# Two hand-outs counted one row group sooner, and raw weights in pieces, in a fused attention and top-1 mixture kernel

## The chip, the core and the metric

The kernel runs on one core of one Trainium2 chip. TensorE multiplies, VectorE (DVE), ScalarE (ACT) and GpSimd (POOL) do the elementwise work, SyncE (SP) and GpSimd issue the transfers between HBM and the core's memory. Each engine and each issuing queue works its own list in order; a row that waits holds everything behind it on that engine. The metric is device time in microseconds (us), the median of several runs; lower is better.

## The reference

Two stages, one behind the other. First an attention over the columns of q, k and v (4 batches of 5056 x 256, the columns of q and k normalised over the 5056 rows), then a mixture of 8 experts over the resulting 20224 tokens, each token going to the one expert with the largest logit.

```
qn = q / (norm(q, axis=1) + 1e-06);  kn = k / (norm(k, axis=1) + 1e-06)
s = kn.T @ qn / tau;  a = softmax(s, -1);  x = v @ a          # per batch, s is 256 x 256
e_idx = argmax(x @ w_gate, axis=1)
gate_w = softmax(x @ w_gate)[e_idx];  eom = sigmoid(x @ w_output_gate)
for e in range(8):
    mask = e_idx == e
    h = relu(x[mask] @ w1[e])                                  # 256 -> 1024
    out[mask] = gate_w[mask] * eom[mask, e] * (h @ w2[e])      # 1024 -> 256
```

## The kernel before

**Stages.** For each of the four batches b, `gram(b)` builds k'q in 20 steps: a step loads two 256 KB pieces into one buffer (tag "qk", six buffers), TensorE multiplies them (s_ps), ACT squares them and DVE adds the squares up; its tail normalises and does the softmax. `mix(b)` then multiplies v with the result, in five row groups (NG = 5) of four steps: v comes in 512 KB pieces (tag "v", four buffers), TensorE transposes it (vt_ps), ACT and DVE split it into a high and a low part (vh, vl), three matmuls give x_ps, and ACT copies that into st (tag "st", four buffers, one per group). `route` decides each token's expert (r_oh and the counts r_ps) and scatters the rows of st from GpSimd into xs_d in HBM, region by expert, eight scatters a group. The mixing of one batch runs beside the gram of the next.

**Units.** Tokens of one expert are worked off in units of 256 (`blocks`): `fetch_x` reads the rows of a unit into xg (which takes a buffer of tag "qk"), `prepare` copies the token numbers (b_id), scales, splits into two f16 parts (xr) and transposes by DMA (xt); then come the matmuls of h_ps with the relu's hb, and those of y_ps, and GpSimd scatters the result to the output. hb shares the tag "raw" with raw weights of the first two ranks. There are 14 early units (FEW = 4 and 10), the others are made when all tokens are counted.

**Hand-outs.** `checkpoint(0)` after the second mixing and `checkpoint(1)` after the third hand out units of the tokens so far; `checkpoint(2)` hands out the rest. The first part of each ranks the experts by their counts (`rank_experts`, the row numbers ri) and issues a *mark*: a small read of xs_d from GpSimd that waits for the scatters before it, and for which every x fetch of these units waits (`open_marks`). The second part makes the tables of units.

**Weights.** `prep(first, end)` works through the ranks: `gather` asks SyncE for the 1 MB of raw weights of one half (w1 or w2) of the rank's expert, and `split` squares it on ACT for a scale (L297), splits it into two f16 parts (L310 on ACT, L311 on DVE) and stores both parts in HBM (wsc, L316). Rank 0 stays in wbuf as well; units from FIRST[1] = 4 on fetch the weights of their rank into wbuf from GpSimd (L825). Raw weights of ranks 0 and 1 have buffers of their own ("raw"), ranks 2 to 7 use those of st. FIRST[r] is the first unit that can have rank r, worked out from the tokens that are sure to be counted.

**Order.** The program is written as generators that the driver at the end steps beside each other: a mixing step, then so many steps of gram (GRATE), of weights (PRATE, MRATE, WRATE) and of units (BRATE). From that the scheduler sets each engine's list. In the third mixing units start at its step OPEN = 10, when the tables were finished at step LATE = 5.

Of the kernel before, what the change touches and what calls it, by code (L numbers as in the profile page):

```python
# [20 lines left out]
P = 128  # L21
# [23 lines left out]
def tile_colnorm_attention_then_top1_moe(  # L45
# [42 lines left out]
    assert 0 < EARLY and LATER >= NHALF  # L88


    sure = [-(-(n * N - E * (BLK - 1)) // BLK) for n in (SOON, B - 1)]
    FIRST = [-(-r * sure[0] // E) for r in range(AHEAD + 1)]
    FIRST += [
        FIRST[AHEAD] - (FIRST[AHEAD] - sure[1]) * (r - AHEAD) // (E - AHEAD) for r in range(AHEAD + 1, E)
# [36 lines left out]
    RLATE = 2  # L131
    GRATE = 1.3
    PRATE = 1.2
    DEEP, LAG, REST = 2, 3, 2
    LATE, OPEN, MARKED = 5, 10, 3
    FAR, NEAR = 5, 1
    BRATE = 0.7
    DRY = 4
    MRATE = 1.2
    WRATE = 0.8  # L140
    units = []
    after = mybir.DependencyInfo(mybir.DependencyClass.Sync, mybir.DependencyReason.DATA)
    xs_d = dr.tile([NSLOT + P, CW], I32, name="xs_d")
# [113 lines left out]
    def prep(first, end):  # L257
        jobs = [(r, half) for r in range(first, end) for half in range(2)]
        raws = []

        def gather():
            r, half = jobs[len(raws)]
            if r > AHEAD:
                raw = wk.tile([P, R, CW], F32, tag="st", name=f"raw{r}_{half}", bufs=STB)
                raw = raw.rearrange("p r w -> p (r w)")[:, :HW1]
            else:
                raw = big.tile([P, HW1], F32, tag="raw", name=f"raw{r}_{half}", bufs=3)
            row = nc.values_load(
                ri[0:1, r : r + 1], engines=[mybir.EngineType.SP], min_val=0, max_val=(E - 1) * P,
                skip_runtime_bounds_check_because="rows of the weights of an expert",  # L270
            )
            if half == 0:
                nc.sync.dma_start(raw, wraw[0][bass.ds(row, P), :])
            else:
                rows = wraw[1][bass.ds(row, P), :].rearrange("(f a) (b d) -> (a b) f d", f=FC, d=C)
                nc.sync.dma_start(raw.rearrange("p (f d) -> p f d", f=FC), rows)
            raws.append(raw)

        for n, (r, half) in enumerate(jobs):
            while len(raws) < min(n + DEEP, len(jobs)):  # L280
                gather()
                yield
            yield from pause(LAG if n == 0 else REST)
            yield from split(raws[n], half, r)

    def split(raw, half, r):

        rows = slice(r * P, (r + 1) * P)
        if r == 0:
            hi, lo = (wbuf[half][:, 0, n * HW1 : (n + 1) * HW1] for n in range(2))  # L290
        else:
            hi = big.tile([P, HW1], F16, tag="sp", name=f"whi{r}_{half}", bufs=1)
            lo = big.tile([P, HW1], F16, tag="sl", name=f"wlo{r}_{half}", bufs=1)
        ss = sm.tile([P, 2], F32, tag="wss", name="wss")
        for i in range(2):
            a = slice(i * HW1 // 2, (i + 1) * HW1 // 2)
            nc.scalar.activation(hi[:, a], raw[:, a], AF.Square, accum_out=ss[:, i : i + 1])  # L297
# [9 lines left out]
        src, dh, dl = raw, hi, lo  # L307
        cuts = [(slice(None), slice(i * HW1 // 2, (i + 1) * HW1 // 2)) for i in range(2)]
        for i, a in enumerate(cuts):
            nc.scalar.activation(dh[a], src[a], AF.Copy, scale=sw)  # L310
            nc.vector.scalar_tensor_tensor(  # L311
                out=dl[a], in0=src[a], scalar=sw, in1=dh[a], op0=ALU.mult, op1=ALU.subtract
            )
            yield
        for n, part in enumerate((hi, lo)):
            nc.sync.dma_start(wsc[half][rows, n * HW1 : (n + 1) * HW1], part)  # L316
# [135 lines left out]
    sowing = []  # L452
    left = [None]

    def mix(b):
        later = None
        turned = []
        sts = {}
# [36 lines left out]
        for j in range(total):  # L495
            g, i = divmod(j, R // 2)
            if j + AHD < total:
                turn(j + AHD)
            if i == 0:
                st = wk.tile([P, R, CW], F32, tag="st", name=f"st{b}_{g}", bufs=STB)  # L500
            vh, vl = turned.pop(0)
            for t in range(2):
                x_ps = ps_x.tile([P, 512], F32, tag="x", name="x_ps")
                for c in range(CC):
                    tsl = slice(t * P, (t + 1) * P)
                    nc.tensor.matmul(x_ps[:, :CW], vh[:, c, tsl], ah[:, c, :], start=c == 0, stop=False)  # L506
                    nc.tensor.matmul(x_ps[:, :CW], vh[:, c, tsl], al[:, c, :], start=False, stop=False)  # L507
                    nc.tensor.matmul(x_ps[:, :CW], vl[:, c, tsl], ah[:, c, :], start=False, stop=c == CC - 1)  # L508
                left[0] = nc.scalar.copy(st[:, 2 * i + t, :], x_ps[:, :CW])  # L509
            sow(1)  # L510
            if i == RLATE and later:
                next(later)
                sowing.append(later)
                sow(1)
            yield
            if i == R // 2 - 1:
                later = route(b, g, st)
                next(later)
        yield
        yield  # L520
        sow(R)
        finish(later)
        yield

# [248 lines left out]
    def checkpoint(ck):  # L773
        last = ck == len(FEW)
        if last:
            close_regions()
        else:
            rank_experts(ck > 0)
        of_rank(rcr, rc)
        open_marks(ck)  # L780
        yield
        if not last:
            a = len(units)
            z = a + FEW[ck]
            table(BLK, FEW[ck], lambda row: [(row[:, a:z], lambda r: r)])
            weights(a, z)
            new = [2] * FEW[ck]
        else:

            few = NHALF - TAIL  # L790
            lead = LATER - few
            mid, end = EARLY + lead, NUNIT - TAIL

            def pairs(a):
                return a[:, mid:end].rearrange("p (h s) -> p h s", s=2)

            def fulls(a):
                return [(a[:, EARLY:mid], lambda r: r[:, :lead]), (pairs(a)[:, :, 0], lambda r: r[:, lead:])]

            def halves(a):  # L800
                return [(pairs(a)[:, :, 1], lambda r: r[:, :few]), (a[:, end:], lambda r: r[:, few:])]

            table(BLK, LATER, fulls)
            table(BLK // 2, NHALF, halves)
            weights(EARLY, NUNIT)
            nc.vector.tensor_copy(more_i, used[0:1, end : end + 1])
            new = [2] * lead + [2, 1] * few + [1] * TAIL
        for nt in new:
            u = len(units)
            units.append(dict(nt=nt, ck=ck, gi=gi[:, u : u + 1], wi=wi[:, u : u + 1], top=max(r for r in range(E) if FIRST[r] <= u)))  # L810
# [153 lines left out]
    def blocks(a, z):  # L964
# [11 lines left out]
        while g <= z:  # L976
# [18 lines left out]
            for fp, steps in enumerate(ORDER):  # L995
# [6 lines left out]
                        y_part(g - 1, part)  # L1002
                if fp == 1:
                    adv("prep", prepare, g + 1 + XP)
                if fp == 0 and a == 0 and g == z - DRY:
                    tc.keep_in_program_order(nc.gpsimd.drain())
                yield
# [14 lines left out]
    for _ in grams[0]:  # L1022
        for _ in range(PER_STAGE):
            next(ahead)
    run = blocks(0, NUNIT - TAIL)
    for b in range(SOON):
        _beside(mix(b) if b else first, (ahead, GRATE))
        while b + 1 not in a_of:
            next(ahead)
    some = checkpoint(0)  # L1030
    next(some)
    preps = prep(0, AHEAD)
    for b in range(SOON, B - 1):
        for i, _ in enumerate(_steps(mix(b), (ahead, GRATE), (preps, PRATE))):
            if i == LATE:
                finish(some)
                opened[0] += 1
            if i >= OPEN:
                next(run)
        while b + 1 not in a_of:  # L1040
            next(ahead)
            next(run)
    finish(preps)
    some = checkpoint(1)
    next(some)
    preps = prep(AHEAD, E)
    for i, _ in enumerate(_steps(mix(B - 1), (run, BRATE), (preps, MRATE))):
        if i == LATE:
            finish(some)
        if i == LATE + MARKED:  # L1050
            opened[0] += 1
    finish(checkpoint(2))
    for i, _ in enumerate(_steps(run, (preps, WRATE))):
        if i == MARKED:
            opened[0] += 1

    more = nc.values_load(
# [34 lines left out]
```

## Time and profile before

| what | us |
|---|---|
| median of three runs | 1208.28 (1202.16 to 1210.1) |
| the profiled execution | 1209.88 |
| its span | 1208.1 |
| mean granted clock of TensorE in it | 0.990 |
| TensorE busy | 1174.4 |
| last matmul of the mixing (L506) starts; units alone behind it | 387.3 |

The span is what the trace covers. Busy time of TensorE takes in matmuls at a lower granted clock, so a stretch can be busy and still lose time. How the span looks in 40 slices (tenths of busy time; the clock in tenths; DMA the busy share of the transfer engines):

```
PE   8999999997997999999999999999999999999997
DVE  7787768788685966566666654555554555555531
ACT  6576656576574555555556443333333444344432
POOL 0003756536565753333444433344444444444433
PEclk9999999999998998999999999999999999999999
DMA  9976888877767898657554436643325534336533
```

A slice is 30 us. The stages of attention fill the first thirteen, the units, from 296 us on, the others beside and behind them.

### The profile page before, as it was taken

The page shows a single profiled execution, that of the slowest core. Times are in us where ns is not written, and L with a number is a line of the kernel's source. Part 1 is how long each engine was busy: PE and PEld are TensorE (multiplying, and loading weights), DVE is VectorE, ACT ScalarE, POOL GpSimd, SP SyncE. Part 2 cuts the span into 40 slices and gives each one's busy share as a digit, 9 for nine tenths or more (in the row PEclk, how much of TensorE's full clock was granted, in tenths as well). Part 3 has the DMA queues.
Part 4 walks back from the last instruction along what each step waited for, and adds up shares of the span by engine and source line. Part 5 has one row for each costly group of instructions (what it writes and reads, how often), then busy time and mean ns, then how long its engine had stood idle before and what let it go on. Part 6 is the DMA issues. An engine that isn't in the chain of part 4 may idle for free.

```text
span 1208.1 us, 28097 instructions
## 1 busy us (share of the span) xinstructions
PE 1174.4 (97%) x10412; PEld 1066.4 (88%) x10412; DVE 748.5 (62%) x2300; ACT 602.3 (50%) x1193; POOL 517.9 (43%) x518
## 2 busy tenths in 40 slices
PE   8999999997997999999999999999999999999997
PEld 7899999887996888888888888888889999999997
DVE  7787768788685966566666654555554555555531
ACT  6576656576574555555556443333333444344432
POOL 0003756536565753333444433344444444444433
PEclk9999999998998999999999999999999999999999
DMA  9976888877767898657554436643325534336533
GB/s 319 330 246 207 301 277 259 295 242 215 212 242 236 223 264 178 150 147 174 148 137 126 112 80 113 182 76 77 72 63 176 112 73 82 79 81 197 168 104 130
DMA packets 186307, 208.56 MB, mean 173 GB/s; under 512 B 121832, under 2 KB 134510, under 8 KB 182200
## 3 DMA queue, kind: packets, MB, share of 16 engines
q1 hardware_dynamic: 145368, 139.41, 42.0%
q0 software_dynamic: 40512, 67.05, 18.9%
q8 instruction: 84, 1.38, 0.5%
q14 instruction: 55, 0.45, 0.1%
q10 hardware_dynamic: 288, 0.26, 0.1%
HBM read 281.84 MB, written 61.41 MB: 284 GB/s over the span
## 4 chain that ended last, share of the span: by engine, by line
PE 87%; DMA 6%; DVE 2%; issue 2%; ACT 1%; SPq 1%; POOL 0%; POOLq 0%; DVEq 0%; ACTq 0%
PE h_ps L919 11%; PE h_ps L921 11%; PE h_ps L920 11%; PE y_ps L942 11%; PE y_ps L943 11%; PE y_ps L944 11%; PE s_ps L366 10%; PE x_ps L506 3%; PE x_ps L508 2%; PE x_ps L507 2%; PE vt_ps L477 2%; DMA wbuf<-wsc,wi 1%; DMA qk<-in_k_dram 1%; DMA raw<-in_moe_w_dram 1%; DMA qk<-in_q_dram 1%
## 5 line engine op out<-in xcount | busy, mean ns | idle before, releaser
L924 DVE SCALAR_TENSOR_TENSOR hb<-h_ps,hb 128x512 f16<-128x512 f32 (+1 forms) x360 | 228.5, 636 | 276.0 <-ACT hb L923 275.1
L923 ACT ACTIVATE hb<-h_ps 128x512 f16<-128x512 f32 (+1 forms) x360 | 197.9, 552 | 364.1 <-PE h_ps L921 362.5
L919 PE MATMUL h_ps<-xt,wbuf 128*128 128x256 f16 (+1 forms) x1440 | 366.5, 262 | 3.0 <-ACT st L509 3.0
L921 PE MATMUL h_ps<-xt,wbuf 128*128 128x256 f16 (+1 forms) x1440 | 366.6, 262 | 0.0
L920 PE MATMUL h_ps<-xt,wbuf 128*128 128x256 f16 (+1 forms) x1440 | 366.5, 262 | 0.0
L942 PE MATMUL y_ps<-wbuf,hb 128*128 128x256 f16 x1296 | 353.3, 273 | 5.0 <-ACT yo L948 2.4
L944 PE MATMUL y_ps<-wbuf,hb 128*128 128x256 f16 x1296 | 353.3, 273 | 0.0
L943 PE MATMUL y_ps<-wbuf,hb 128*128 128x256 f16 x1296 | 353.3, 273 | 0.0
L825 POOL DMA_INDIRECT wbuf<-wsc,wi x172 | 177.8, 1034 | 404.5 <-PE h_ps L921 365.2
L598 POOL DMA_INDIRECT xs_d<-st,r_si x160 | 168.1, 1051 | 199.2 <-DVE r_d L550 101.9
L954 POOL DMA_INDIRECT out_dram<-yo,b_id x162 | 165.4, 1021 | 69.2 <-issue 42.3
L366 PE MATMUL s_ps<-qk 128*128 128x256 f32 x640 | 152.4, 390 | 5.8 <-DMA qk<-in_q_dram 3.9
L920 PEld LDWEIGHTS <-wbuf 128*128 128x128 f16 x1440 | 141.0, 98 | 16.9 <-issue 3.2
L919 PEld LDWEIGHTS <-wbuf 128*128 128x128 f16 x1440 | 142.1, 99 | 14.1
L921 PEld LDWEIGHTS <-wbuf 128*128 128x128 f16 x1440 | 141.1, 98 | 13.3
L943 PEld LDWEIGHTS <-hb 128*128 128x128 f16 x1296 | 126.8, 98 | 19.3 <-issue 5.6
L366 PEld LDWEIGHTS s_ps<-qk 128*128 128x128 f32 x640 | 121.4, 196 | 21.2 <-DMA qk<-in_k_dram 3.9
L944 PEld LDWEIGHTS <-hb 128*128 128x128 f16 x1296 | 126.8, 98 | 14.9
L942 PEld LDWEIGHTS <-hb 128*128 128x128 f16 x1296 | 126.8, 98 | 14.3
L354 DVE TENSOR_TENSOR acc<-acc,sq 128x1024 f32<-128x1024 f32 x76 | 92.9, 1223 | 46.8 <-ACT sq L353 45.4
L880 ACT ACTIVATE xr<-xg,b_sx 128x256 f16<-128x256 f32 x162 | 74.6, 502 | 66.8 <-DVE b_sx L233 46.4
L353 ACT ACTIVATE sq<-qk 128x1024 f32<-128x1024 f32 x76 | 80.3, 1060 | 53.0 <-DMA qk<-in_k_dram 44.8
(191 smaller groups left out, 1448.8 us busy)
## 6 DMA issues: line engine op xcount, KB each, us to landing
xg<-xs_d SPq DMA_DIRECT2D x72, 272.0 KB
qk<-in_q_dram SPq DMA_DIRECT2D x75, 256.0 KB
qk<-in_k_dram SPq DMA_DIRECT2D x75, 256.0 KB
v<-in_v_dram SPq DMA_DIRECT2D x32, 512.0 KB
raw<-in_moe_w_dram SPq DMA_DIRECT2D x16, 1024.0 KB
wsc<-whi SPq DMA_DIRECT2D x14, 512.0 KB
wsc<-wlo SPq DMA_DIRECT2D x14, 512.0 KB
v<-in_v_dram SPq DMA_DIRECT2D x8, 480.0 KB
```

The source lines that it names most:

```text
L366: nc.tensor.matmul(s_ps[:, c, :], kt[:, 1, t, c * P : (c + 1) * P], qt[:, 0, t, :], start=st == 0 and t0 == 0 and t == 0 and c == 0 and n ...
L598: ins = nc.gpsimd.indirect_dma_start(out=xs_d[:, :], out_offset=bass.IndirectOffsetOnAxis(ap=si[:np_, t : t + 1], axis=0), in_=st[:np_, t, ...
L825: nc.gpsimd.indirect_dma_start(out=wbuf[half][:, at_of(u), :], out_offset=None, in_=wsc[half][:end, :], in_offset=bass.IndirectOffsetOnAxi ...
L919: nc.tensor.matmul(hp, w1s[:, 0, c, fs], xh, start=fi == 0 and c == 0, stop=False, **KWM)
L920: nc.tensor.matmul(hp, w1s[:, 0, c, fs], xl, start=False, stop=False, **KWM)
L921: nc.tensor.matmul(hp, w1s[:, 1, c, fs], xh, start=False, stop=fin, **KWM)
L923: nc.scalar.activation(hh, h_ps[:, :, :w], AF.Relu)
L924: nc.vector.scalar_tensor_tensor(out=hb[:, 1, 2 * fp : 2 * fp + 2, :w], in0=h_ps[:, :, :w], scalar=0.0, in1=hh, op0=ALU.max, op1=ALU.subtract,
L942: nc.tensor.matmul(y_ps[:, t, :], hb[:, 0, f, tsl], w2s[:, 0, f, :], start=st, stop=False, **KWM)
L943: nc.tensor.matmul(y_ps[:, t, :], hb[:, 0, f, tsl], w2s[:, 1, f, :], start=False, stop=False, **KWM)
L944: nc.tensor.matmul(y_ps[:, t, :], hb[:, 1, f, tsl], w2s[:, 0, f, :], start=False, stop=fin, **KWM)
L954: ins = nc.gpsimd.indirect_dma_start(out=out[:, :], out_offset=bass.IndirectOffsetOnAxis(ap=un["id"][:, t : t + 1], axis=0), in_=un["yo"][ ...
```

## The change

- `sure` (from which FIRST follows) takes off one batch's last row group, 960 tokens. FIRST goes from 0, 4, 11, 18, 25, 32, 39, 46 to 0, 4, 11, 17, 23, 30, 36, 42.
- `mix` takes a hook. In the second and third mixing it ranks the experts when the last row group's third step runs, and issues the mark at the end of the mixing, ahead of the last group's scatters. The hand-outs so count four of the five groups of their last batch.
- The tables are finished at step 1 of the next mixing (LATE) and units start at step 3 (OPEN). Weights of rank 0 start in the second mixing at step 18 (HOOKED), those of rank 1 in the third one at step 18; rank 2 and later wait 22 steps more (REST_AT), and pause four steps a half (SLOW).
- Raw weights come in two transfers a half, the f16 parts go out in two stores each, with steps of other work between. Ranks 2 to 7 use buffers of tag "v" in place of "st".
- `blocks` calls `fetch_x` at every step.

```diff
-    sure = [-(-(n * N - E * (BLK - 1)) // BLK) for n in (SOON, B - 1)]
+    sure = [-(-(n * N - (N - (NG - 1) * GROUP) - E * (BLK - 1)) // BLK) for n in (SOON, B - 1)]
...
-    DEEP, LAG, REST = 2, 3, 2
-    LATE, OPEN, MARKED = 5, 10, 3
+    DEEP, LAG, REST, SLOW = 2, 4, 1, 4
+    LATE, OPEN, MARKED, HOOKED = 1, 3, 3, 18
...
-    BRATE = 0.7
+    REST_AT = 22
+    BRATE = 0.72
...
-    MRATE = 1.2
-    WRATE = 0.8
+    MRATE = 1.8
+    WRATE = 1.0
...
             if r > AHEAD:
-                raw = wk.tile([P, R, CW], F32, tag="st", name=f"raw{r}_{half}", bufs=STB)
-                raw = raw.rearrange("p r w -> p (r w)")[:, :HW1]
+                parts = [
+                    ld.tile([P, 4, C], F32, tag="v", name=f"raw{r}_{half}_{i}", bufs=VB).rearrange("p t c -> p (t c)")
+                    for i in range(2)
+                ]
             else:
                 raw = big.tile([P, HW1], F32, tag="raw", name=f"raw{r}_{half}", bufs=3)
+                parts = [raw[:, i * HW1 // 2 : (i + 1) * HW1 // 2] for i in range(2)]
...
+            for i, part in enumerate(parts):
+                if half == 0:
+                    nc.sync.dma_start(part, rows[:, i * HW1 // 2 : (i + 1) * HW1 // 2])
...
+                yield
...
-            yield from pause(LAG if n == 0 else REST)
+            yield from pause(LAG if n == 0 else SLOW if r > AHEAD + 1 else REST)
...
-        for n, part in enumerate((hi, lo)):
-            nc.sync.dma_start(wsc[half][rows, n * HW1 : (n + 1) * HW1], part)
+            for n, part in enumerate((hi, lo)):
+                nc.sync.dma_start(wsc[half][rows, n * HW1 + a.start : n * HW1 + a.stop], part[:, a])
+            yield
...
+                if g == NG - 1 and hook:
+                    next(hook)
...
         sow(R)
+        if hook:
+            next(hook)
         finish(later)
...
         of_rank(rcr, rc)
+        if not last:
+            yield
         open_marks(ck)
...
+                adv("x", fetch_x, got["prep"] + QKB)
...
     for b in range(SOON, B - 1):
-        for i, _ in enumerate(_steps(mix(b), (ahead, GRATE), (preps, PRATE))):
+        for i, _ in enumerate(_steps(mix(b, hand[1]), (ahead, GRATE))):
+            if i < HOOKED:
+                due += PRATE
+                while due >= 1.0:
+                    due -= 1.0
+                    next(preps, None)
+            else:
+                if i == HOOKED:
+                    finish(preps)
+                    preps = chain(prep(AHEAD, AHEAD + 1), pause(REST_AT), prep(AHEAD + 1, E))
+                next(preps)
             if i == LATE:
-                finish(some)
+                finish(hand[0])
                 opened[0] += 1
             if i >= OPEN:
-                next(run)
+                some += 1.0 if i < OPEN + FAR + XP + 1 + NEAR else BRATE
```

The matmuls stay the same, in number and shape; the lists of the engines change order. Three places show it.

The first is GpSimd's queue at the end of the second mixing; st_4 is its last row group, the st_0 behind it the first of the third mixing. Before:

```order
L598 DMA xs_d<-st_3_2251,r_si 163968x272 x8
L598 DMA xs_d<-st_4_2439,r_si 163968x272 x8
L615 DMA mark<-xs_d 128x1
L598 DMA xs_d<-st_0_2766,r_si 163968x272 x8
L598 DMA xs_d<-st_1_2954,r_si 163968x272 x8
```

After:

```order
L608 DMA xs_d<-st_3_2251,r_si 163968x272 x8
L625 DMA mark<-xs_d 128x1
L608 DMA xs_d<-st_4_2439,r_si 163968x272 x8
L608 DMA xs_d<-st_0_2778,r_si 163968x272 x8
L608 DMA xs_d<-st_1_3020,r_si 163968x272 x8
```

The mark has moved ahead of eight scatters. In SyncE's queue in the same place, raw_0 and raw_1 are the two halves of rank 0's raw weights, qk_15 the loads of gram step 15 of the last batch. Before:

```order
L342 DMA qk_15_3165<-in_q_dram 128x512
L342 DMA qk_15_3165<-in_k_dram 128x512
L268 TENSOR_LOAD ri
L273 ISA
L273 DMA raw_0_2793<-in_moe_w_dram 128x2048
L268 TENSOR_LOAD ri
L276 ISA
L276 DMA raw_1_2833<-in_moe_w_dram 128x8x256
L342 DMA qk_16_3243<-in_q_dram 128x512
L342 DMA qk_16_3243<-in_k_dram 128x512
```

After (the last of four fetches of token rows, and what follows it; the four pieces of raw weights stand a little ahead, behind qk_10):

```order
L851 TENSOR_LOAD gi
L855 ISA
L855 DMA xg<-xs_d 128x544
L348 DMA qk_11_3037<-in_q_dram 128x512
L348 DMA qk_11_3037<-in_k_dram 128x512
L348 DMA qk_12_3073<-in_q_dram 128x512
L348 DMA qk_12_3073<-in_k_dram 128x512
L471 DMA v_3_2_3537<-in_v_dram 128x1024
L471 DMA v_4_0_3641<-in_v_dram 120x1024
L321 DMA wsc_85<-wbuf_155 128x1024 x2
L348 DMA qk_13_3149<-in_q_dram 128x512
L348 DMA qk_13_3149<-in_k_dram 128x512
```

Rank 0's raw weights have gone from behind step 15 to behind step 10; the fetches of token rows, which came behind step 19, come ahead of step 11, and rank 0's stores (wsc) between the later steps, two of them ahead of 13, two ahead of 14, one ahead of 16 and three ahead of 17.

The second place is DVE in the first row group of the third mixing, around r_oh, on which r_ps waits. Before (the tb_ rows and elist make the table of units):

```order
L552 SCALAR_TENSOR_TENSOR r_val<-r_d,c_113 128x64
L571 CAST st_0_2766<-ids 128x8
L701 TENSOR_REDUCE tb_res<-tb_pr 128x4 x2
L554 TENSOR_REDUCE r_mv<-r_val 128x8
L714 SCALAR_TENSOR_TENSOR tb_ex<-tb_res,tb_g_3035 128x4
L704 SCALAR_TENSOR_TENSOR tb_sl<-jf,tb_res 128x4
L556 TENSOR_TENSOR r_oh<-r_val,r_mv 128x64
```

After:

```order
L581 CAST st_0_2778<-ids 128x8
L489 TENSOR_TENSOR vl<-vt_ps,vh 128x512
L564 TENSOR_REDUCE r_mv<-r_val 128x8
L871 COPY b_id<-xg 128x2
L875 TENSOR_REDUCE b_mx<-xg 128x2
L571 TENSOR_REDUCE r_se<-r_d 128x8
L566 TENSOR_TENSOR r_oh<-r_val,r_mv 128x64
L871 COPY b_id<-xg 128x2
L875 TENSOR_REDUCE b_mx<-xg 128x2
L232 TENSOR_SCALAR b_mx<-b_mx 128x2
L489 TENSOR_TENSOR vl<-vt_ps,vh 128x512
```

The first rows of unit 0 (b_id, which reads a fetched xg) now stand ahead of r_oh, and unit 1's ahead of the next vl; units 2 and 3 follow within ten rows. In the last mixing, four b_id stand ahead of the first vl in the same way.

The third place is SyncE in the last mixing, at the raw weights of rank 2. Before:

```order
L268 TENSOR_LOAD ri
L276 ISA
L276 DMA raw_1_5208<-in_moe_w_dram 128x8x256
L839 TENSOR_LOAD gi
L843 ISA
L843 DMA xg<-xs_d 128x544
L839 TENSOR_LOAD gi
L843 ISA
L843 DMA xg<-xs_d 128x544
L885 DMA_TRANSPOSE xt<-xr_3657 128x4x128 x4
L316 DMA wsc_86<-whi_1_4850 128x2048
L316 DMA wsc_86<-wlo_1_4851 128x2048
```

After:

```order
L855 DMA xg<-xs_d 128x544
L321 DMA wsc_85<-whi_0_4392 128x1024 x2
L471 DMA v_3_2_5076<-in_v_dram 128x1024
L321 DMA wsc_85<-wlo_0_4393 128x1024 x2
L471 DMA v_4_0_5218<-in_v_dram 120x1024
L471 DMA v_4_2_5377<-in_v_dram 120x1024
L321 DMA wsc_86<-whi_1_4599 128x1024 x2
L321 DMA wsc_86<-wlo_1_4600 128x1024 x2
L897 DMA_TRANSPOSE xt<-xr_3296 128x4x128 x2
L273 TENSOR_LOAD ri
L280 ISA
L280 DMA raw_0_0_5686<-in_moe_w_dram 128x1024
```

The raw weights of rank 2 (raw_1_5208 is the second half of them, raw_0_0_5686 the first piece of their first half) have gone behind the stores of rank 1 (wsc) and behind the last loads of v.

More of the change, by code (lines that the diff above doesn't have):

```diff
@@ L263, in gather @@
             if r > AHEAD:
-                raw = wk.tile([P, R, CW], F32, tag="st", name=f"raw{r}_{half}", bufs=STB)
-                raw = raw.rearrange("p r w -> p (r w)")[:, :HW1]
+                parts = [
+                    ld.tile([P, 4, C], F32, tag="v", name=f"raw{r}_{half}_{i}", bufs=VB).rearrange("p t c -> p (t c)")
+                    for i in range(2)
+                ]
             else:
                 raw = big.tile([P, HW1], F32, tag="raw", name=f"raw{r}_{half}", bufs=3)
+                parts = [raw[:, i * HW1 // 2 : (i + 1) * HW1 // 2] for i in range(2)]
+            raws.append(parts)
             row = nc.values_load(
@@ L271, in gather @@
             )
[L272 to L277, printed above, removed]
+            rows = wraw[half][bass.ds(row, P), :]
+            for i, part in enumerate(parts):
+                if half == 0:
+                    nc.sync.dma_start(part, rows[:, i * HW1 // 2 : (i + 1) * HW1 // 2])
+                else:
+                    nf = FC // 2
+                    of = rows.rearrange("(f a) (b d) -> (a b) f d", f=FC, d=C)[:, i * nf : (i + 1) * nf, :]
+                    nc.sync.dma_start(part.rearrange("p (f d) -> p f d", f=nf), of)
+                yield
         for n, (r, half) in enumerate(jobs):
             while len(raws) < min(n + DEEP, len(jobs)):
-                gather()
-                yield
-            yield from pause(LAG if n == 0 else REST)
+                yield from gather()
+            yield from pause(LAG if n == 0 else SLOW if r > AHEAD + 1 else REST)
             yield from split(raws[n], half, r)
@@ L296, in split @@
             a = slice(i * HW1 // 2, (i + 1) * HW1 // 2)
-            nc.scalar.activation(hi[:, a], raw[:, a], AF.Square, accum_out=ss[:, i : i + 1])
+            nc.scalar.activation(hi[:, a], raw[i], AF.Square, accum_out=ss[:, i : i + 1])
             yield
@@ L305, in split @@
         root2(tot, KW, sw, invw[:, half, r : r + 1])
[L307 to L310, printed above, removed]
+        for i in range(2):
+            a = slice(i * HW1 // 2, (i + 1) * HW1 // 2)
+            nc.scalar.activation(hi[:, a], raw[i], AF.Copy, scale=sw)
             nc.vector.scalar_tensor_tensor(
-                out=dl[a], in0=src[a], scalar=sw, in1=dh[a], op0=ALU.mult, op1=ALU.subtract
+                out=lo[:, a], in0=raw[i], scalar=sw, in1=hi[:, a], op0=ALU.mult, op1=ALU.subtract
             )
+            for n, part in enumerate((hi, lo)):
+                nc.sync.dma_start(wsc[half][rows, n * HW1 + a.start : n * HW1 + a.stop], part[:, a])
             yield
-        for n, part in enumerate((hi, lo)):
-            nc.sync.dma_start(wsc[half][rows, n * HW1 : (n + 1) * HW1], part)
         if half == 1:
@@ L453, in tile_colnorm_attention_then_top1_moe, with mix @@
     left = [None]
-    def mix(b):
+    def mix(b, hook=None):
         later = None
@@ L1025, in tile_colnorm_attention_then_top1_moe @@
     run = blocks(0, NUNIT - TAIL)
+    hand = [checkpoint(n) for n in range(len(FEW))]
+    preps = prep(0, AHEAD)
     for b in range(SOON):
-        _beside(mix(b) if b else first, (ahead, GRATE))
+        hook = hand[0] if b == SOON - 1 else None
+        for i, _ in enumerate(_steps(mix(b, hook) if b else first, (ahead, GRATE))):
+            if hook and i >= HOOKED:
+                next(preps)
         while b + 1 not in a_of:
             next(ahead)
-    some = checkpoint(0)
-    next(some)
-    preps = prep(0, AHEAD)
+    due = some = 0.0
     for b in range(SOON, B - 1):
-        for i, _ in enumerate(_steps(mix(b), (ahead, GRATE), (preps, PRATE))):
+        for i, _ in enumerate(_steps(mix(b, hand[1]), (ahead, GRATE))):
[4 more added lines that the diff above has]
+                    next(preps, None)
+            else:
+                if i == HOOKED:
+                    finish(preps)
+                    preps = chain(prep(AHEAD, AHEAD + 1), pause(REST_AT), prep(AHEAD + 1, E))
+                next(preps)
             if i == LATE:
-                finish(some)
+                finish(hand[0])
                 opened[0] += 1
             if i >= OPEN:
-                next(run)
+                some += 1.0 if i < OPEN + FAR + XP + 1 + NEAR else BRATE
+                while some >= 1.0:
+                    some -= 1.0
+                    next(run)
         while b + 1 not in a_of:
@@ L1042, in tile_colnorm_attention_then_top1_moe @@
             next(run)
[L1043 to L1046, printed above, removed]
     for i, _ in enumerate(_steps(mix(B - 1), (run, BRATE), (preps, MRATE))):
         if i == LATE:
-            finish(some)
+            finish(hand[1])
         if i == LATE + MARKED:
@@ L1053, in tile_colnorm_attention_then_top1_moe @@
     for i, _ in enumerate(_steps(run, (preps, WRATE))):
-        if i == MARKED:
+        if i == 3:
             opened[0] += 1
```

## The prediction, made before the changed kernel ran

> **What bounds the kernel now.** I read the page first: busy shares and the chain that ended last.
>
> ```profile
> PE 1174.4 (97%) x10412; PEld 1066.4 (88%) x10412; DVE 748.5 (62%) x2300; ACT 602.3 (50%) x1193; POOL 517.9 (43%) x518
> ...
> PE 87%; DMA 6%; DVE 2%; issue 2%; ACT 1%; SPq 1%; POOL 0%; POOLq 0%; DVEq 0%; ACTq 0%
> ```
>
> TensorE is the bound almost everywhere. The change removes no matmul, so it can only move the places where TensorE stands. Those I found with a table by stretches (PE busy, count, granted clock, DMA share, GB/s):
>
> ```profile
> 238.00:250.00 12.00, 7.91 (x46) 0.86 0.80 291
> 250.00:274.00 24.00, 24.00 (x176) 1.00 0.78 247
> 274.00:296.00 22.00, 14.84 (x112) 0.84 0.82 211
> 366.00:384.00 18.00, 10.44 (x64) 0.81 0.85 259
> 420.00:430.00 10.00, 8.36 (x77) 1.00 0.99 227
> ...
> 430.00:1184.00 754.00, 753.75 (x7311) 1.00 0.51 126
> ```
>
> Behind 430 us nothing is to be won: 753.75 of 754 us are busy. Four stretches ahead of it lose time. I count idle time plus busy time times the missing share of the clock: 4.1 + 1.1 = 5.2 us at 238, 7.2 + 2.4 = 9.5 at 274, 7.6 + 2.0 = 9.5 at 366 and 1.6 at 420. That is 25.8 us, the whole stake. The waits of TensorE in these stretches name the releasers:
>
> ```profile
> PE r_ps L576 <- DVE r_oh L556: 5.3, 1, 5.3
> PE r_ps L576 <- ACT st L509: 4.1, 1, 4.1
> ...
> PE h_ps L919 <- ACT st L509: 3.0, 1, 3.0
> PE y_ps L942 <- ACT yo L948: 2.4, 1, 2.4
> PE vt_ps L477 <- DVE vl L483: 2.1, 1, 2.1
> PE y_ps L942 <- DMA wbuf<-wsc,wi: 1.6, 1, 1.6
> ```
>
> The names on ACT and DVE are not the causes. The chain of waits shows what each had been standing behind. At 238 us:
>
> ```profile
> 229.36 0.60 DVE vl L483
> 231.09 8.47 DMA raw<-in_moe_w_dram
> 239.59 2.19 ACT wbuf L297 x4
> ...
> 242.50 0.28 ACT st L509
> ```
>
> Rank 0's raw weights are asked for at 231.09 and land at 239.56; the squares of L297 stand on ACT ahead of the copy into st, so ACT, and then TensorE, wait for the weights. At 366 us it is SyncE's queue (its rows in order of time), held first by the longest of its waits at L276:
>
> ```profile
> SPq L276 <- DMA xs_d<-st,r_si: 18.5, 2, 9.4
> ...
> 358.11 0.39 SPq L276 DMA_DIRECT2D raw<-in_moe_w_dram  x1
> 359.05 1.23 SPq L843 DMA_DIRECT2D xg<-xs_d  x2
> 360.39 9.85 SPq L885 DMA_TRANSPOSE xt<-xr  x4
> 370.34 0.53 SPq L316 DMA_DIRECT2D wsc<-whi  x1
> ...
> 370.34 6.91 DMA wsc<-whi
> 377.33 0.13 ACT whi L297
> ```
>
> The raw weights of rank 2 go into an st buffer whose scatters have not landed. SyncE stands 9.4 us; the rows of units, their transposes and the stores of rank 1 come late behind it, and ACT's next squares (377.33) wait for that store, with the copies into st behind them.
>
> **The change part by part.** I add up against the profiled execution: 1209.88 us, its span 1208.1 and 1.8 around it. The median is 1208.28, so 1.6 below; I carry that difference over.
>
> *Hand-out 0 earlier.* The mark (a small read that the fetch of token rows waits for) moves from behind the last group's scatters to before them:
>
> ```profile
> 223.30 0.97 POOL L598 DMA_INDIRECT xs_d<-st,r_si  x1 [0.30 <-issue]
> ...
> 234.10 1.00 POOL L598 DMA_INDIRECT xs_d<-st,r_si  x1 [0.30 <-issue]
> 235.40 1.00 POOL L598 DMA_INDIRECT xs_d<-st,r_si  x1 [0.30 <-issue]
> 242.07 0.61 POOL L615 DMA_DIRECT2D mark<-xs_d  x1 [5.66 <-DMA xs_d<-st,r_si]
> ...
> SPq L843 <- DMA mark<-xs_d: 2.0, 1, 2.0
> ...
> L843 SPq DMA_DIRECT2D xg<-xs_d x4: 343/343/348, 249.4 to 260.5; - x4
> L859 DVE COPY b_id<-xg x4: 161/166/340, 252.6 to 265.0; 128x2 int32<-128x2 int32 x4
> ```
>
> The last scatter ahead of the new place ends at 224.27; with the same 5.66 us to landing the mark is issued at about 229.9 and read by about 232.5 (0.61 and the 2.0 of SyncE). A fetch takes 252.6 − 249.4 = 3.2 us, so the first token rows are there at about 235.7. The ranking is done a group sooner as well, by one group's scatters (235.40 − 223.30 is some 12 us), so rank 0's raw weights are asked for near 219 and land near 227.5 by the 8.47 us of today. The wait at 238 goes: −5.2. But DVE's queue now has b_id of units 0 and 1 ahead of r_oh and vl of mix(2) group 0, where it had none. That group's r_oh is what TensorE's 4.1 us wait stood in front of; it is due around 235.7 when no weights are late. With the rows landing just then, plus a reduction of 0.7 and small ones, I take a wait of 1.8 (0 if the mark lands sooner; 6 if it takes the 5.66 of a landing once more). Behind it on DVE stand all vl of this mixing, and TensorE waits for those.
>
> *The rows' buffers.* The four fetches stand in SyncE's queue ahead of gram step 11 and wait for the mark; they take four of the six buffers that gram's q and k use. The steps 12 to 19 share two until ACT and DVE have read the rows. A step's TensorE work and its square:
>
> ```profile
> 250.35 1.73 PE s_ps L366 x8
> ...
> L353 ACT ACTIVATE sq<-qk 128x1024 f32<-128x1024 f32 x76 | 80.3, 1060 | 53.0 <-DMA qk<-in_k_dram 44.8
> ```
>
> One buffer's round is two issues (0.4 each), the 3.2 us of a fetch and 1.73 of reading, some 5.8; two buffers give a step each 2.9 us, against 1.73. In the new order of TensorE four steps (14 to 17) come back to back without other work: 4 × 1.2 = 4.8, say +5.0. Ends: 0, if the rows are read early and the buffers come back; 10.5, if nine steps lose 1.17 each. Rank 0's stores, in four pieces each half's pair, stand between these loads in SyncE's queue and wait for ACT and DVE; I price them inside that end.
>
> *The DVE backlog at 274.* In that stretch rank 0's split (1.20 each) runs beside gram's tail:
>
> ```profile
> 276.14 1.68 DVE rn L392
> ...
> 279.96 1.20 DVE wbuf L311
> ...
> 284.86 1.67 DVE rn L397
> ```
>
> The two pieces of the split that fall into it move ahead of it (2.4), and the first unit's matmuls start before the last gram step's tail instead of behind it, so that TensorE has other work there. Gram's tail itself stays. Of 9.5 I take −5.0; ends −9.5 and 0.
>
> *Ranks 2 to 7 in v's buffers.* Raw rank 2 no longer waits for scatters and stands behind the last v loads; SyncE passes the units' rows and transposes ahead of it. The wait of 9.4 goes, and with it the stretch at 366: −9.0; ends −9.5 and −4, if DVE's late vl (2.1) and ACT's yo (2.4) have other reasons as well. Later ranks are ready later, but need not be sooner: steady units hide them. A unit costs about 10 us (753.75 us for some 73 units' worth behind 430), and a rank's work comes once in five or six of them.
>
> *Hand-out 1 earlier.* The same head-of-line wait: four b_id of units 4 to 7 come ahead of the first vl of mix(3). +2.5; ends 0 and 6, as above.
>
> *The weights' fetch at 420.* GpSimd's queue has fetches of rank 1 ahead of group 0's and 1's scatters, so the scatters start late, and the fetches of units 6 and 7 stand behind 8 scatters each time (1.3 apart by the rows above, 10.4 us a group). Today that costs 1.6:
>
> ```profile
> 417.37 5.52 DMA wbuf<-wsc,wi
> ```
>
> I take 1.5 more; ends −1.6 and +5.5, a whole fetch.
>
> *At nothing:* raw loads and stores in two pieces each (the same bytes; SyncE's 0.4 us an issue, hidden since its queue mostly waits), x fetches at more places (they fill free buffers), the third hand-out's literal step (the same number 3).
>
> Sum: −5.2 + 1.8 + 5.0 − 5.0 − 9.0 + 2.5 + 1.5 = −8.4, so 1201.5 for a profiled execution and **1199.9** for the median.
>
> A rule of the Trainium skill bears on the new short waits. Ahead of it the rows: the clock fell to 0.86 behind a wait of 4.1 us, and to 0.81 in the stretch at 366, whose longest wait was 3.0; it stayed at 1.00 behind 1.6. The page "TensorE: Matmul & The Clock Gate" says (Part 1, What's actually happening) that the gate halves the clock after an idle window of about 3.4 us. The stretch at 366 fell with shorter waits in a row, so the trace is stricter than the rule. By the rule new waits of 1.8 and 2.5 cost no clock and the sum stays; by the row at 366 each would cost up to 2.0 more, and the sum would be −4.4.
>
> **Rivals.** *The cover holds* (rows land before DVE asks, buffers come back in time): the two +terms of hand-outs and the 5.0 fall to nothing, 1.5 stays and the backlog loses 7: −5.2 − 7 − 9 + 1.5 = −19.7, so 1188.6. For it: the mark's path has only two DMAs in a row; against: my own times land just at the need.
> *The stalls only move* (not what it says): the scatters' backlog shows up again at the end of mix(3), where TensorE's wait at 420 grows by a fetch and the 366 stretch keeps its yo and vl waits: −5.2 + 1.8 + 5 − 3 − 5 + 2.5 + 5.5 = +1.6, 1209.9 with the carried −1.6. For it: GpSimd and SyncE carry the same transfers in the same 200 us.
> *Slower:* SyncE between steps 11 and 19 becomes the bound. Its stores of rank 0 wait for ACT and DVE between the q and k loads, four places, at the mean of today's row:
>
> ```profile
> SPq L316 <- ACT whi L310: 22.1, 8, 5.3
> ```
>
> 22.1 / 8 = 2.8 each, 11.2 in all, on top of the 10.5 of two buffers: 21.7 in place of 5.0; gram's tail then comes late and the backlog's −5 goes too: −8.4 + 16.7 + 5 = +13.3, so 1221.6. It decides the sign beyond 1% from about 20 us of loss in those steps. Against it: ACT has slack there, and the stores follow work that moved ahead too.
>
> **How the numbers follow.** About 1% (12 us) is what a measurement of this kernel can tell from no change: under 1196.2 is faster, above 1220.4 slower. The forecast has 0.42 (its own range 1192 to 1208, and 0.4 of it under 1196), the cover 0.23, the moved stalls 0.18, the slower rival 0.17. Faster: 0.17 + 0.23 = 0.40; slower 0.17; the same 0.43. The range leaves out half of the slower rival and the best of the cover: 1185 to 1218.
>
> **What would show it.** Right: no wait at L276's successor for scatters, the stretch from 360 to 384 full, raw rank 0 asked for near 219; a wait of TensorE of 1 to 3 us near 236 on r_ps or vl, with DVE's b_id waiting for xg; gram steps 14 to 17 some 2.9 us apart. Wrong: SyncE rows between steps 11 and 19 with waits over 3 us each (slower), or TensorE full from 235 to 265 (cover). The prediction falls altogether if time is lost behind 430 us, through ranks that come late.

## The result, and the profile after

The changed kernel takes 1219.0 us (median of four runs, 1215.6 to 1224.5); the kernel before took 1208.0 beside it. The ratio is 1.0101, with a 95% interval of 1.0072 to 1.0131: slower by about 11 us, and a ratio of 1 lies outside the interval. The profiled execution took 1218.5 us, span 1216.8, granted clock 0.992.

The page after, busy shares and the chain that ended last:

```profile
PE 1178.3 (97%) x10412; PEld 1065.5 (88%) x10412; DVE 740.9 (61%) x2300; ACT 604.7 (50%) x1193; POOL 521.4 (43%) x518
...
PE 65%; DMA 6%; issue 4%; POOL 2%; ACT 1%; DVE 1%; SPq 0%; POOLq 0%; ACTq 0%; DVEq 0%
```

As many matmuls as before, and the same share of busy time. The chain is put down to an engine for 79% of the span only, so its 65% for TensorE can't be held against the 87% of before; the stretches carry the reading. They (PE busy, count, granted clock, DMA share, GB/s) show where the time went; the borders are those of the prediction's terms in the new execution:

```profile
222.00:246.00 24.00, 22.05 (x148) 0.93 0.88 300
246.00:282.00 36.00, 26.62 (x158) 0.95 0.85 260
282.00:306.00 24.00, 21.25 (x193) 1.00 0.44 126
306.00:342.00 36.00, 32.11 (x269) 0.95 0.84 278
342.00:390.00 48.00, 44.16 (x381) 0.96 0.69 208
...
402.00:438.00 36.00, 32.02 (x285) 0.95 0.53 157
```

Idle time plus busy time times the missing clock, as in the prediction: 3.5, 10.7, 2.8, 5.5, 5.6 and 5.6 us, 33.7 in all, where the four bad stretches before had 25.8. Four bad stretches have become six, and the one that loses most is new: 246 to 282 us, in the last batch's gram. The waits of TensorE over the whole execution name it:

```profile
PE s_ps L372 <- DMA qk<-in_k_dram: 7.9, 5, 2.4
PE vt_ps L483 <- DVE vl L489: 5.3, 4, 1.6
PE h_ps L931 <- DMA wbuf<-wsc,wi: 4.0, 2, 2.8
PE s_ps L372 <- DMA qk<-in_q_dram: 3.8, 1, 3.8
PE x_ps L512 <- ACT st L515: 3.3, 5, 2.0
...
PE k_ps L387 <- DVE st L580: 1.5, 1, 1.5
```

The 3.8 of q is the kernel's start; the five waits for k, 7.9 us, did not exist before. With the 1.5 of k_ps, which stands in gram's tail at 279.77, and 1.3 of clock they make up the 10.7 us. The chain of waits there, in order of time:

```profile
245.03 5.40 DMA qk<-in_k_dram
...
252.99 6.62 DMA qk<-in_k_dram
259.61 0.14 issue
259.75 1.98 PE s_ps L372 x8
...
261.79 0.33 SPq L348
...
262.17 5.51 DMA qk<-in_k_dram
```

These are the loads of k of the steps 13, 15 and 17: they take 5.4 to 6.6 us. The two in between, from their issue to the square on ACT that waits for them, take 8.0 (step 14) and 4.6 (step 16). A load goes out when a buffer comes free: TensorE has read step 15 at 261.73, and the loads of step 17 start at 261.79. The token rows that hold four buffers had landed long ago; the copies that read them start at 264.4:

```profile
L892 ACT ACTIVATE xr<-xg,b_sx x8: 492/492/509, 264.4 to 280.1; 128x256 f16<-128x256 f32 x8
...
L871 DVE COPY b_id<-xg x4: 166/170/170, 233.8 to 237.6; 128x2 int32<-128x2 int32 x4
```

So the rows fetched at 230 sit in gram's buffers for over 30 us, through the rest of gram up to its last steps.

Something else stands between these loads as well, the stores of rank 0. SyncE waits twice for ACT in front of them, 6.3 and 4.2 us:

```profile
SPq L321 <- ACT wbuf L316: 10.5, 2, 6.3
```

These waits run mostly beside the waits for a buffer. Counted from the end of the reading that frees the buffer, the loads of the steps 13, 14 and 16 went out 1.6, 1.4 and 0.6 us late behind stores, those of 15, 17 and 18 within 0.1 us. So the stores can have cost some 3.6 us here at most, an estimate from these rows.

The other new waits are in the last mixing. The second hand-out: GpSimd issues the mark, and DVE's first b_id stands for the fetch behind it, with vl in its queue (the number in brackets is the idle time of the row's engine before it):

```profile
319.24 0.59 POOL L625 DMA_DIRECT2D mark<-xs_d  x1 [6.12 <-issue]
...
323.99 0.17 DVE L871 COPY b_id<-xg 128x2 int32<-128x2 int32 x1 [4.64 <-DMA xg<-xs_d]
...
324.66 0.68 DVE L489 TENSOR_TENSOR vl<-vt_ps,vh 128x512 fp32r<-128x512 f32 x1
```

And where rank 2's weights had stalled the kernel before, the chain of waits shows two transfers in turn:

```profile
347.95 6.77 DMA out_dram<-yo,b_id
354.81 0.17 DVE b_id L871
...
363.45 6.77 DMA raw<-in_moe_w_dram
370.33 1.15 ACT whi L304 x2
...
373.90 0.30 ACT st L515
```

A b_id of a later unit waits for its buffer, whose old numbers an output scatter still reads; that scatter (347.95) had waited on GpSimd behind a weight fetch that stood 9.85 us, as GpSimd's rows in order of time show. Then ACT's squares of rank 2 (L304) wait for its raw weights, ahead of the copies into st: the same pattern as at 238 us before, two ranks later.

```profile
345.28 1.06 POOL L837 DMA_INDIRECT wbuf<-wsc,wi  x1 [9.85 <-DVE vl L489]
...
347.95 0.97 POOL L966 DMA_INDIRECT out_dram<-yo,b_id  x1 [0.31 <-issue]
...
420.00 1.06 POOL L608 DMA_INDIRECT xs_d<-st,r_si  x1 [0.30 <-issue]
421.37 1.04 POOL L837 DMA_INDIRECT wbuf<-wsc,wi  x1 [0.30 <-PE y_ps L956]
```

The last two rows are the end of the last group's eight scatters and the weight fetch behind them, for which h_ps waits 2.8 us.

### The profile page after: what moved, and what is told of

Its sections match the earlier page's. It is cut to its first block, busy times and chain, and to the rows that moved or that the text cites. A ratio compares the mean times of both kernels' runs of the same rounds, so it can differ in the third digit from the quotient of the medians.

```text
span 1216.8 us, 28229 instructions
## 1 busy us (share of the span) xinstructions
PE 1178.3 (97%) x10412; PEld 1065.5 (88%) x10412; DVE 740.9 (61%) x2300; ACT 604.7 (50%) x1193; POOL 521.4 (43%) x518
## 4 chain that ended last, share of the span: by engine, by line
PE 65%; DMA 6%; issue 4%; POOL 2%; ACT 1%; DVE 1%; SPq 0%; POOLq 0%; ACTq 0%; DVEq 0%
PE h_ps L931 11%; PE h_ps L933 11%; PE h_ps L932 10%; PE y_ps L954 10%; PE y_ps L956 10%; PE y_ps L955 10%; DMA wbuf<-wsc,wi 2%; DMA qk<-in_k_dram 1%; POOL xs_d L608 1%; DMA out_dram<-yo,b_id 1%; PE s_ps L372 1%; DMA xs_d<-st,r_si 1%; POOL out_dram L966 1%; DMA raw<-in_moe_w_dram 1%; PE x_ps L514 0%
## 5 line engine op out<-in xcount | busy, mean ns | idle before, releaser
L608 POOL DMA_INDIRECT xs_d<-st,r_si x160 | 172.2, 1076 | 200.8 <-DVE r_d L560 99.7
L512 PE MATMUL x_ps<-ah,vh 128*128 128x272 f32 x320 | 102.8, 324 | 3.9 <-ACT st L515 3.3
```

Source lines behind the costliest of these rows:

```text
L608: ins = nc.gpsimd.indirect_dma_start(out=xs_d[:, :], out_offset=bass.IndirectOffsetOnAxis(ap=si[:np_, t : t + 1], axis=0), in_=st[:np_, t, ...
```

## The experiments

Several causes were set against each other: the fetched rows hold gram's buffers (A); units that start early crowd DVE and ACT (B); SyncE stands for the mark (C in e1 and e7), or the hand-outs and the later weights cost by themselves (C in e2 and e3, D in e8). Ratios are to the kernel before on the same chip.

**First round, on another chip.** Four kernels ran where the kernel before took 1263 us. TensorE there stands often between 120 and 480 us without a wait that the profile shows (last section), so that only ratios are used.

*e1: own buffers.* Three of the first four units' rows lie in the third raw buffer, one in that of the f16 weights.

```diff
+    spare = []
...
+        if u == 0:
+            spare.append(big.tile([P, HW1], F32, tag="raw", name="xg012", bufs=3).bitcast(I32))
+        if u < 3:
+            xg = spare[0][:, u * 2 * CW : (u + 1) * 2 * CW].rearrange("p (t w) -> p t w", t=2)
+        elif u == 3:
+            xg = big.tile([P, HW1], F16, tag="sp", name="xg3", bufs=1).bitcast(I32)[:, : 2 * CW].rearrange("p (t w) -> p t w", t=2)
+        else:
+            xg = ld.tile([P, 2, TS, C], F32, tag="qk", name="xg", bufs=QKB)
...
```

> The changed kernel, but the token rows of the first four units do not take gram's buffers: three lie in the free third buffer of the raw weights, one in that of the f16 weights. Theory A (the four early fetches hold four of gram's six buffers until ACT and DVE read them, and steps 12 to 19 starve): the TensorE waits for q and k between 246 and 282 us, some 10 us of the changed kernel, go, and the time falls from 1219 to 1209 to 1212. Rival B (the loss is the units' early work on ACT and DVE beside the mixing, which delays vl and st): the waits for q and k go but as much comes back on vl, st and hb, and the time stays above 1216. Rival C (SyncE stands for the mark, whatever buffers there are): the waits for q and k stay, 1217 to 1220.

Measured: 1262.6 against 1263.1, ratio 0.9987 (0.9949 to 1.0024). The waits for q and k are gone but for the start. By the ratio this points to A, but the changed kernel itself had not run on this chip.

*e2: late opening.* `LATE, OPEN` 5 and 10 again in place of 1 and 3.

> The changed kernel, but the tables are finished at step 5 and units start at step 10 as before; the earlier hand-outs, the pieces and v's buffers stay. Theory A: the fetches stand behind gram's last loads, gram does not starve, and the rest of the gains stands: 1203 to 1210. Rival B (early units as such): also faster, but the waits on vl and st between 294 and 375 us go too, 1200 or less. Rival C (the hand-out itself, or the raw weights in v's buffers, costs): stays at 1214 or above.

Measured: 0.9998 (0.9964 to 1.0032). No wait for q or k behind the start either. It fits A, and C as well, since the fetches with their wait for the mark now stand behind gram's loads; the absolute times expected can't be read on this chip.

*e3: hand-outs as before,* with the changed raw weights: the driver, FIRST and the steps of the kernel before; the driver's line for the weights, against the kernel before, is

```diff
-    preps = prep(AHEAD, E)
+    preps = chain(prep(AHEAD, AHEAD + 1), pause(REST_AT), prep(AHEAD + 1, E))
```

> The hand-outs, FIRST and the driver's steps of the kernel before, with the changed kernel's raw weights (two pieces a half, two stores, third rank and later in v's buffers behind the last mixing, its rates). Theory A (moving the third rank's raw weights off st takes the stall at 366 us away and costs nothing): 1198 to 1203, the stall at 238 us stays. Rival C (the late ranks or the pieces cost as much as they win): 1206 to 1212.

Measured: 1.0024 (0.9996 to 1.0051). The 1206 to 1212 of the rival would be some 0.998 to 1.003, so by its number this is the rival's case; the repeats e10 and e13 come out lower.

*e4: raw weights in st again.*

```diff
-                parts = [
-                    ld.tile([P, 4, C], F32, tag="v", name=f"raw{r}_{half}_{i}", bufs=VB).rearrange("p t c -> p (t c)")
-                    for i in range(2)
-                ]
+                raw = wk.tile([P, R, CW], F32, tag="st", name=f"raw{r}_{half}", bufs=STB)
...
```

> The changed kernel, but raw weights of the third rank and later lie in st's buffers again, fetched in two pieces and as late as in the changed kernel. If their place in time is what takes the 366 us stall away: same as the changed kernel, 1216 to 1222. If v's buffers are what takes it away: the wait for scatters in SyncE's queue is back and the time is 5 to 10 us more, 1224 to 1229.

Measured: 1.0142 (1.0081 to 1.0203). By the ratio this is the second case (1224 to 1229 would be 1.013 to 1.017), but the interval also holds the changed kernel's 1.0101 of the other chip, and the mechanism of the second case is missing: SyncE waits for scatters at these rows only 1.2 us. So the long wait of before seems to be avoided by the later place alone; whether v's buffers win anything besides stays open.

This kernel keeps the four rows in gram's buffers, as the changed kernel does, and it is the only one of the four in which TensorE waits for k:

```profile
PE s_ps L370 <- DMA qk<-in_k_dram: 14.3, 4, 7.0
```

**Second round, on a chip like the first** (the kernel before 1207.7). *e5: the changed kernel again.*

> The changed kernel itself, as the measure for the others on this chip. Both theories: 0.5 to 1.5% above the kernel before.

Measured: 1221.0, ratio 1.0116 (1.0088 to 1.0143).

*e6: own buffers again.*

> The changed kernel with token rows of the first four units outside gram's buffers, again, beside the changed kernel on the same chip. Theory A (buffers): 8 to 12 us less than the changed kernel. Rivals B and C: within 3 us of it.

Measured: 1205.6, ratio 0.9987 (0.9970 to 1.0005), the same ratio as on the other chip and 15.4 us under the changed kernel beside it, more than the 8 to 12 expected. Units start as early as in the changed kernel, so B falls as the main cause. But the edit moved more than the buffers: in SyncE's list the fetches now stand behind the loads of step 17 in place of step 10, and in its trace SyncE does not stand for the first mark. So this run alone does not part A from C.

*e7: two early fetches.* Two units' rows, not four, are fetched ahead of gram step 11. SyncE still stands for the mark there, 8.0 us against 8.3 in e5.

```diff
-            adv("x", fetch_x, got["prep"] + QKB)
+            adv("x", fetch_x, got["prep"] + (2 if g == a == 0 else QKB))
...
                     adv("prep", prepare, n + 1)
+                    if a == 0:
+                        adv("x", fetch_x, got["prep"] + 2)
```

> The changed kernel, but two token row fetches instead of four stand ahead of gram step 11, still waiting for the mark there; the other two follow as units 0 and 1 are read. Gram keeps four buffers. Theory A (buffers): the TensorE waits for q and k fall from 10 us to 4 or less, time 4 to 10 us below the changed kernel. Rival C (SyncE standing for the mark ahead of step 11 is the cost): waits and time stay within 3 us of it.

Measured: 1212.1, ratio 1.0038 (1.0027 to 1.0049), 8.9 us under the changed kernel. TensorE's waits for k, 5.8 us in e5, are

```profile
PE s_ps L372 <- DMA qk<-in_k_dram: 3.5, 2, 2.9
```

The gram stretch in e5 (four buffers held), e7 (two) and e6 (none), each from its own table:

```profile
246.00:282.00 36.00, 28.43 (x161) 0.91 0.87 270
```

```profile
246.00:282.00 36.00, 32.34 (x234) 1.00 1.01 284
```

```profile
246.00:282.00 36.00, 34.58 (x268) 1.00 0.87 228
```

Lost: 10.1, 3.7 and 1.4 us. Two buffers given back recover 6.4 of 8.7 while SyncE's wait for the mark stays where it was; so A holds and C, as the main cause, falls. What is left between e7 and e6, 2.3 us, can be the two other buffers or SyncE; no run parts these.

Two things limit this. The stores wait less in e7 too (2.8 us for ACT against 7.3 in e5), so that a part of the 6.4 can be theirs. And C has a price in the stretch ahead, 222 to 246 us: e5 loses 5.0 there, e7 4.9 and e6 2.2, and the longest wait for k in e7, 2.9 us, is for step 11, the first load behind the mark. The profiled executions of e5 and e6 are 13.2 us apart: 8.7 lie in gram's stretch and 2.8 in this one; the later stretches gain and lose.

*e8: own buffers, second hand-out as before* (no hook in the third mixing, tables at step 5, units open at step 8).

> As the own buffers, and the second hand-out undone as well (after the third mixing, tables at step 5, units at step 8, as before). Theory D (the second early hand-out costs by itself: b_id ahead of vl waiting for the mark, GpSimd's scatters late): 4 to 8 us less than with own buffers alone. Rival: it is neutral or a gain, 0 to 5 us more.

Measured: 1208.2, ratio 1.0000 (0.9987 to 1.0013), 2.5 us above e6: D falls. The early second hand-out is a small gain, or none. The wait that it was blamed for is not tied to it, though: in e8 DVE's b_id still stands 5.5 us for a fetch, and the stretch still loses 7.3 us, where e6 loses 7.8:

```profile
306.00:342.00 36.00, 30.20 (x248) 0.95 0.76 249
```

**Third round.** *e9 to e13.* e11 is e9 again, e12 is e6 again, e10 and e13 are e3 again; e9 and e10 had met a chip of the pausing kind once more (kernel before 1270.4). e9 queues DVE's b_id of units 4 to 13 behind the last vl written before it, on top of own buffers:

```diff
+            vls.append(nc.vector.tensor_tensor(out=vl, in0=t_ps, in1=vh.bitcast(F32), op=ALU.subtract).ins)
...
-        copied = nc.vector.tensor_copy(idt[:, :nt], xr[:, :, C])
+        with tc.issue_after(vls[-1]) if FEW[0] <= u < EARLY else contextlib.nullcontext():
+            copied = nc.vector.tensor_copy(idt[:, :nt], xr[:, :, C])
```

> As the own buffers for the first four units' rows, and the first DVE row of units 4 to 13 (b_id, which waits for the second mark's fetch) queued behind the vl that were written before it, so that it no longer stands ahead of the last mixing's first vl. Theory E (the waits on vl and st between 300 and 335 us, 7 us there, come from this b_id standing for the fetch): the wait of 3 us on vl near 312 goes and the time is 3 to 8 us under the own buffers alone (0.9987 of the kernel before), so 0.992 to 0.996. Rival F (DVE and ACT are simply full there): 0.997 to 1.000.

> Again the hand-outs and steps of the kernel before with the changed kernel's raw weights, in the hope of a chip on which the first run's many short pauses of TensorE do not stand. Theory: the stall at 366 us goes (9.5 us), the one at 238 us stays: 0.992 to 0.997 of the kernel before. Rival (the late ranks or the pieces give it back): 1.000 or more.

Measured there: 1.0014 (0.9973 to 1.0054) and 0.9983 (0.9949 to 1.0018); neither decides anything.

> The b_id rows queued behind vl on top of own buffers, again, beside own buffers alone on the same chip (next run). Theory E: 3 to 8 us under own buffers alone, where TensorE does not stand in short pauses of its own. Rival F: within 2 us of it.

> Own buffers alone, as the measure for the run before this: 0.9987 of the kernel before, as in both runs so far.

> Hand-outs and steps of the kernel before with the changed raw weights. Theory: 0.992 to 0.997 of the kernel before, since the 9.5 us stall at 366 us goes and nothing else is touched. Rival (late ranks or pieces give it back): 1.000 or more.

Measured, kernel before 1209.2: e11 1202.5, ratio 0.9937 (0.9918 to 0.9956); e12 1204.8, 0.9968 (0.9946 to 0.9989); e13 1206.6, 0.9960 (0.9946 to 0.9975).

e12's interval holds the 0.9987 expected, and e13 lies in the range of its theory. e11 is 2.3 us under e12, below the 3 to 8 expected, and the two intervals overlap. The wait itself does go: the waits of DVE from 300 to 330 us in own buffers alone (e6),

```profile
DVE b_id L880 <- DMA xg<-xs_d: 7.9, 3, 7.0
```

are gone in e11, where vl waits for TensorE instead:

```profile
DVE vl L491 <- PE x_ps L516: 4.9, 2, 3.9
...
PE x_ps L514 <- ACT st L517: 4.2, 1, 4.2
```

But TensorE then stands 4.2 us for a copy into st. The stretch in e12 and in e11:

```profile
306.00:342.00 36.00, 29.48 (x243) 0.95 0.73 246
```

```profile
306.00:342.00 36.00, 30.91 (x241) 0.86 0.70 240
```

It loses 8.0 us in e12 and 9.4 in e11, and from 306 to 438 us the two lose nearly the same, 16.1 and 15.8. So E is right about the cause of the vl wait, but the traces do not show that taking it away is worth anything; the 2.3 us between the medians stay without a place.

e13 moves the weights and their rates, not the hand-outs, and gains 2.6 us by the medians, not the 9.5 of the stall that it removes. Where it was lost instead, stretches and waits of e13:

```profile
342.00:390.00 48.00, 45.00 (x415) 1.00 0.83 231
390.00:402.00 12.00, 7.24 (x66) 0.91 0.48 111
...
PE y_ps L954 <- DMA wbuf<-wsc,wi: 5.0, 2, 4.8
```

3.0 us are left of the stretch itself, and 5.4 have moved behind it, to a weight fetch that GpSimd issues behind the last scatters.

e11 beats both kernels: 0.9937 of the one before, some 1.6% under the changed one by the ratios (0.9937 / 1.0101).

## Why the prediction was wrong

The forecast was 1199.9 (1185 to 1218), the measured time 1219.0. Term by term, the loss of the term's stretch after, less that before, in us:

| term | forecast | measured |
|---|---|---|
| hand-out 0 (5.2 before, 3.5 after) | −3.4 | −1.7 |
| the rows' buffers (0 before, 10.7 after) | +5.0 | +10.7 |
| DVE backlog (9.5 before, 2.8 after) | −5.0 | −6.7 |
| hand-out 1 (0.2 before, 5.5 after) | +2.5 | +5.3 |
| rank 2 (9.5 before, 5.6 after) | −9.0 | −3.9 |
| weights' fetch (1.6 before, 5.6 after) | +1.5 | +4.0 |
| sum | −8.4 | +7.7 |

The profiled executions differ by 1218.5 − 1209.9 = 8.6, so the table holds nearly all of it. The sign of every term is right; the sizes are not.

- **The rows' buffers**, the step that failed most. The forecast took the 3.2 us landing of one lone fetch for the loads' round. Beside rank 0's stores and the v loads the three in the chain took 5.4 to 6.6 (the transfer engines are full: their share, the number before the last, is 1.02 in the second row below). With 0.8 of issue and 1.7 to 2.0 of reading a round is 8 to 9 us and a step on two buffers 4 or more, not 2.9. The sign that it named, the steps 14 to 17 some 2.9 us apart, came as 3.9, 3.7 and 4.4; their waits for k were 1.6, 2.0, 1.7 and 2.4 where it had 1.2 each, 7.7 in place of 4.8. The rest of the 10.7, the clock (1.3) and the wait of k_ps (1.5), stood in no term. The upper end, 10.5, was passed. e5, e7 and e6 show that it is mainly the buffers; the stores that stood between the loads, priced "inside that end", can have some 3.6 us of it. Two narrower stretches of the changed kernel, for this and for the clock:

```profile
234.00:246.00 12.00, 10.05 (x59) 0.86 0.98 334
...
258.00:270.00 12.00, 6.12 (x22) 0.92 1.02 308
```

- **Rank 2.** The wait for scatters went as forecast, and the stretch still lost 5.6, so the gain of 3.9 just misses the range of 4 to 9.5. The prediction asked what is late next only of vl and yo; late next were the output scatter that held b_id's buffer, and rank 2's own raw weights ahead of st on ACT. In e13, with the hand-outs of before, much of the loss came back as a weight fetch. A stall's length was booked as its worth.
- **Hand-out 1** was priced at 2.5 from a guess like the first one's. The mark came at 319.24, 7.1 us after the last scatter's start, and DVE stood 4.6 us. That the early mark makes this wait is not shown: e8, with the mark as before, keeps it. e11 shows that the order of DVE's list can take it away, and that TensorE then waits for the copies into st instead.
- **The weights' fetch**: right in kind (GpSimd issued one at 421.37, behind eight scatters, and TensorE stood for it), near the upper end.
- **Hand-out 0** came as told: raw weights asked for at 216.9 (219 forecast), the mark at 228.1 (229.9), first b_id at 233.8 (235.7). The wait named near 236 on r_ps or vl came in pieces of 0.4 and 1.2 us.
- **The clock.** By the page "TensorE: Matmul & The Clock Gate" of the Trainium skill (Part 1, What's actually happening) the gate halves the clock after an idle window of about 3.4 us. The trace disagrees with the reading that shorter waits cost no clock: between 234 and 246 us no wait of TensorE was longer than 1.2, and the granted clock was 0.86 (0.50 from 238 to 240). The reading from the row at 366, up to 2.0 more for each hand-out, was the right one: 1.5 us of clock at 222 to 246, 1.6 at 306 to 342.

Of the rivals, the slower one named the right place, and its sign came too: SyncE's rows stood 6.3 and 4.2 us for ACT between these steps. But half of its 21.7 us were the stores, at 11.2, and the whole stretch lost 10.7. That its 1221.6 lies near the 1219.0 is luck: what came was a sum of five overruns, of which none alone turns the forecast's sign. The case of the moved stalls was right for rank 2. That the cover would hold was wrong for gram. Behind 450 us nothing was lost, as forecast: 741.5 of 742 us are busy.

## What to carry to other kernels

A buffer that is taken sooner is held sooner: before fetching earlier into a shared pool, look up when its *reader* runs, not when the fetch lands, and price the loads that then rotate over the rest with the landing time of that stage, with its traffic, not of a quiet one. A stall removed from one chain is worth no more than the distance to the next late thing, so name that for each removed wait and bound the gain with it; where an engine's list is in order, an instruction that waits for a new early transfer is a new stall for everything behind it.

## What the runs showed of the hardware

The experiments ran in four sets, two of them on chips where the same kernel before took 1263 and 1270 us in place of 1208. Nearly all of the difference lies between 120 and 480 us: in e3, on such a chip, TensorE is busy for 319.1 of these 360 us at a clock of 0.91, in e6 for 342.3 at 0.99, while ahead of them it is 113.4 and 113.5 of 120 us. Two stretches of e3 (PE, PEld, DVE, ACT, POOL busy, granted clock, DMA share, GB/s):

```profile
420.00:450.00 30.00, 20.00 (x138) 13.02 (x135) 12.67 (x62) 4.86 (x11) 18.34 (x19) 0.80 0.32 90
480.00:510.00 30.00, 30.00 (x278) 26.91 (x277) 19.27 (x61) 16.48 (x31) 11.11 (x11) 1.00 0.81 206
```

In the first, TensorE stands again and again for 0.3 to 1.1 us with nothing that the profile shows it waiting for, and its clock is 0.80, while every other engine has less to do as well; from 480 us on both are as on the other chips. What makes these pauses no run shows. A small difference between kernels can get lost in them: the same kernel had a ratio of 1.0014 there (e9) and of 0.9937 on another chip (e11).
